# One inverse matmul per frequency instead of two: the filter product crossed over by VectorE and summed on GpSimd

## The chip, the cores and the metric

The kernel runs on one core of a Trainium2 chip. The metric is the device time of one execution in microseconds (us), the lower the better. Most executions of a kernel agree within 0.3%. A ratio in this text is the mean time of one kernel's fast runs over the mean of the other's fast runs of the same rounds, so it is not quite the ratio of the medians quoted beside it.

PE is TensorE's matmul stream, PEld its weight loads, DVE is VectorE, ACT is ScalarE, POOL is GpSimd, SP is the queue that issues most DMAs.

## The reference

Two parts in a row: a frequency-domain filter along the sequence, then a feed-forward block with a scaled sigmoid gate.

```python
# x: (8, 3008, 256), filt_r and filt_i: (1505, 256)
X = np.fft.rfft(x, axis=1)
Y = X * (filt_r + 1j * filt_i)
y = np.fft.irfft(Y, n=3008, axis=1)            # (8, 3008, 256)
h = y.reshape(24064, 256) @ w_in               # 2048 columns
g = h / (1 + np.exp(-beta * h))
out = g @ w_out                                # (24064, 256)
```

## The kernel before

The transform of length 3008 = 47 x 64 is done with matmuls in four stages per batch: s1 (47-point), s2 (64-point, with twiddles), the filter product and s3 (inverse 64-point), s4 (inverse 47-point). A complex number lies as real part in partitions 0 to 63 and imaginary part in 64 to 127.

Batch 0 is transformed alone. From then on the feed-forward matmuls of batch b-1 are the main stream, in 752 steps (two w_in matmuls of 512 columns, four w_out matmuls of 256), and the units of batch b's transform are sprinkled into it by a fixed plan.

```python
hpsum = tile_pool(bufs=2, PSUM); opsum = tile_pool(bufs=3, PSUM)   # w_in result; output accumulators
fpsum = tile_pool(bufs=3, PSUM)                                    # all transform results
...
def s2(i):                                   # two frequencies, 2*i and 2*i+1
    ps = fpsum.tile([P, 2, D], F32)
    # two matmuls of 256 columns into ps, weights t2
    p_t = pqpool.tile([P, 2, D], BF16)
    q_t = pqpool.tile([P, 2, D], BF16)
    nc.vector.tensor_tensor(p_t[:], ps[:], fr_sb[:, k0 : k0 + 2, :], ALU.mult)
    nc.vector.tensor_tensor(q_t[:], ps[:], fi_sb[:, k0 : k0 + 2, :], ALU.mult)
def s3(i):
    ps = fpsum.tile([P, 2, D], F32)
    for e in range(2):                       # two matmuls per frequency, summed in PSUM
        for tab, src, first in ((t3p, p_t, True), (t3q, q_t, False)):
            nc.tensor.matmul(ps[:, e, :], lhsT=tab[...], rhs=src[:, e, :], start=first, stop=not first)
    evac(st["z"][:, kk : kk + 2, :], ps[:], both)   # ScalarE in batch 0, else VectorE
def s23(i):
    if i < NK // 2: s2(i)()
    if i >= 1:      s3(i - 1)()
...
spans = ((0.0, 0.20), (0.32, 0.60), (0.74, 1.0))   # shares of a batch's steps for s1, s2+s3, s4
...
for s in range(len(steps) + LAG):
    # w_in matmuls of step s; gate on ScalarE
    # the transform units planned for step s
    # w_out matmuls of step s-2 into acc; after 16 steps (a block of 512 tokens):
    nc.vector.tensor_copy(ost[...], acc[h][...])   # two copies of 128x512
```

The table t3q holds the same weights as t3p, turned by a quarter and with the sign of the conjugated half. That is how the cross terms of the complex product get to the right half and sign: the second matmul does it.

## Time and profile before

888.59 us (median of the 4 runs beside the changed kernel, 887.69 to 890.02).

| engine | busy us | share of 885.9 us |
|---|---|---|
| PE | 783.4 | 88% |
| ACT | 543.2 | 61% |
| DVE | 414.1 | 47% |
| POOL | 38.2 | 4% |

The page of the profile: the busy line, the busy tenths in 40 equal slices for PE and VectorE, and the chain that ended last with its first line by source.

```profile
span 885.9 us, 14752 instructions
PE 783.4 (88%) x5860; PEld 551.3 (62%) x5953; DVE 414.1 (47%) x691; ACT 543.2 (61%) x789; POOL 38.2 (4%) x79
...
PE   0023599999999999999999999999999999999997
...
DVE  6844556545463438335563437435463438331101
...
PE 77%; DMA 14%; DVE 4%; issue 2%; ACT 1%; SPq 1%; DVEq 0%; ACTq 0%
```

From about 110 us PE is at 90% or more to the end, and the chain is PE for 77%. So the body is bound by the matmul stream. VectorE's 47% is an average over stages, and its slices go up and down between 3 and 8 as long as there are transforms. The stage that the change touches is looked at alone in the next two views, for batch 3. First the timeline of VectorE (start us, us, engine, line, operation, shapes; in brackets the idle time in front of it):

```profile
337.44 0.69 DVE L333 TENSOR_TENSOR p_t<-ps_3530,fr_sb 128x512 bf16<-128x512 f32 x1 [0.50 <-PE ps_3530 L324]
338.05 0.68 DVE L334 TENSOR_TENSOR q_t<-ps_3530,fi_sb 128x512 bf16<-128x512 f32 x1
338.64 0.68 DVE L282 CAST z<-ps_3537 128x512 bf16<-128x512 f32 x1
339.83 0.69 DVE L333 TENSOR_TENSOR p_t<-ps_3562,fr_sb 128x512 bf16<-128x512 f32 x1 [0.50 <-PE ps_3562 L324]
```

An instruction takes 0.68 us, but the next one starts 0.60 us after it: they overlap by 0.08. A unit of this stage is one pair of frequencies: its products on VectorE and one z copy. A unit comes every 2.39 us, VectorE needs 1.8 to 1.9 of it and idles 0.50. It has some room here, not half of its time. Second, the waits of PE between 329 and 371 us, this stage (who waited for whom: us in total, times, longest):

```profile
PE ps_3427 L324 <- DMA a_3320<-d_3048: 0.8, 1, 0.8
PE acc L474 <- DVE ost L486: 0.2, 1, 0.2
```

PE waits for nothing of VectorE's but 0.2 us.

### The profile page before, as it was taken

How to read it: one execution, taken by the hardware profiler on the slowest of the kernel's cores; microseconds unless marked ns; L12 is line 12 of the kernel's file. 1: busy time of each engine (PE TensorE's matmuls, PEld its weight loads, DVE VectorE, ACT ScalarE, POOL GpSimd, SP SyncE). 2: the span in 40 equal slices, each digit the busy share in tenths (PEclk: the TensorE clock that was granted, in tenths of full speed). 3: DMA queues.
4: the chain of work that ended last, by engine and by line, in shares of the span. 5: the costliest groups of instructions: out<-in, count | busy, mean ns of one | idle time of the engine just before them, and what ended most of it. 6: DMA issues, size and time to landing. Idle time of an engine off the chain costs nothing.

```text
span 885.9 us, 14752 instructions
## 1 busy us (share of the span) xinstructions
PE 783.4 (88%) x5860; PEld 551.3 (62%) x5953; DVE 414.1 (47%) x691; ACT 543.2 (61%) x789; POOL 38.2 (4%) x79
## 2 busy tenths in 40 slices
PE   0023599999999999999999999999999999999997
PEld 0001466676676767677676767777676767777665
DVE  6844556545463438335563437435463438331101
ACT  1311365666667665776667665676667665777775
POOL 5010010001000000001000000000000000000000
PEclk9999799999999999999999999999999999999999
DMA  9967465517523382507524371504523152501011
GB/s 212 221 146 182 125 120 159 137 37 155 148 85 112 64 197 62 154 26 156 147 79 119 63 198 61 155 26 112 155 79 106 56 150 62 153 26 48 25 48 48
DMA packets 94869, 97.70 MB, mean 110 GB/s; under 512 B 6544, under 2 KB 84880, under 8 KB 94800
## 3 DMA queue, kind: packets, MB, share of 16 engines
q1 hardware_dynamic: 90432, 83.38, 31.5%
q0 software_dynamic: 4368, 13.37, 10.4%
q8 instruction: 46, 0.75, 0.3%
q14 instruction: 23, 0.19, 0.1%
HBM read 60.30 MB, written 49.81 MB: 124 GB/s over the span
## 4 chain that ended last, share of the span: by engine, by line
PE 77%; DMA 14%; DVE 4%; issue 2%; ACT 1%; SPq 1%; DVEq 0%; ACTq 0%
PE acc L474 34%; PE hps L440 31%; DMA fr_sb<-in_filt_r_dram 5%; DVE ost L486 2%; DMA ws<-in_moe_w_out_dram 1%; DMA d_676<-a_738 1%; DMA d_1769<-a_1985 1%; DMA d_3048<-a_3264 1%; DMA d_5606<-a_5822 1%; DVE q_t L334 1%; DMA d_319<-a_347 1%; DMA zz<-d_677 1%; DMA d_676<-a_838 1%; DMA d_319<-a_375 1%; SPq L259 1%
## 5 line engine op out<-in xcount | busy, mean ns | idle before, releaser
L449 ACT ACTIVATE gT<-hps,beta_sb 128x512 bf16<-128x512 f32 x752 | 515.8, 687 | 252.6 <-PE hps L440 217.4
L474 PE MATMUL acc<-wout_sb,gT 128*128 128x256 bf16 x3008 | 456.7, 273 | 5.1 <-DVE ost L486 0.9
L440 PE MATMUL hps<-y,win_sb 128*128 128x512 bf16 (+7 forms) x1635 | 429.6, 351 | 0.5 <-DVE y L284 0.3
L474 PEld LDWEIGHTS <-gT 128*128 128x128 bf16 x3008 | 287.2, 98 | 143.3 <-issue 6.8
L440 PEld LDWEIGHTS <-win_sb 128*128 128x128 bf16 x1728 | 165.0, 98 | 25.6 <-issue 1.7
L486 DVE COPY ost<-acc 128x512 f32<-128x512 f32 x94 | 60.2, 681 | 123.1 <-PE acc L474 123.0
L386 PEld LDWEIGHTS <-zz 96*128 96x128 bf16 x512 | 36.5, 102 | 35.5 <-DMA zz<-d_320 7.7
L303 PEld LDWEIGHTS <-t_129 94*96 94x96 bf16 x128 | 16.7, 132 | 58.3 <-issue 53.1
L324 PEld LDWEIGHTS <-t_131 128*128 128x128 bf16 x192 | 19.2, 100 | 40.6 <-issue 20.9
L80 POOL DMA_DIRECT2D xg<-in_x_dram x32 | 17.2, 536 | 570.2 <-PE ps_6948 L303 85.1
L303 PE MATMUL ps_343<-xg,t_129 94*96 94x512 bf16 x1 | 0.6, 586 | 31.2 <-ACT a_333 L280 31.2
L349 PEld LDWEIGHTS <-t3q 128*128 128x128 bf16 x192 | 19.1, 99 | 8.7 <-issue 5.6
L349 PEld LDWEIGHTS <-t3p 128*128 128x128 bf16 x192 | 19.1, 99 | 5.7 <-DVE p_t L333 0.8
L81 POOL DMA_DIRECT2D xg<-in_x_dram x32 | 16.4, 513 | 1.6 <-DMA xg<-in_x_dram 1.6
L303 PE MATMUL ps_351<-xg,t_129 94*96 94x512 bf16 x1 | 0.6, 586 | 14.8 <-DVE a_333 L282 14.8
L137 DVE TENSOR_TENSOR r<-u,r 128x1536 f32<-128x1536 f32 x6 | 10.5, 1758 | 0.2
L280 ACT ACTIVATE a_347<-ps_351 96x512 bf16<-96x512 f32 x1 | 0.6, 592 | 16.1 <-PE ps_351 L303 16.1
L165 PE MATMUL tp<-ident,t_129 94*96 94x94 bf16 x1 | 0.3, 312 | 11.3 <-DVE t_129 L161 11.3
L138 ACT ACTIVATE t_131<-r 128x1536 bf16<-128x1536 f32 x2 | 3.0, 1483 | 10.7 <-DVE r L137 10.7
L324 PE MATMUL ps_397<-a_389,t_131 128*128 128x256 bf16 x2 | 0.6, 397 | 9.0 <-DMA a_389<-d_319 9.0
L264 DVE TENSOR_SCALAR wout_sb<-ws,rbeta_sb 128x256 bf16<-128x256 f32 x16 | 4.6, 348 | 7.7 <-DMA ws<-in_moe_w_out_dram 7.7
L138 ACT ACTIVATE t3p<-r 128x1536 bf16<-128x1536 f32 x2 | 3.0, 1483 | 7.5 <-DVE r L137 7.5
(1158 smaller groups left out, 622.3 us busy)
## 6 DMA issues: line engine op xcount, KB each, us to landing
out_dram<-ost SPq DMA_DIRECT2D x47, 512.0 KB, 2.9
xg<-in_x_dram POOLq DMA_DIRECT2D x32, 320.0 KB, 5.3
fr_sb<-in_filt_r_dram SPq DMA_DIRECT2D x16, 192.0 KB, 6.9
fi_sb<-in_filt_i_dram SPq DMA_DIRECT2D x16, 192.0 KB, 8.6
ws<-in_moe_w_out_dram SPq DMA_DIRECT2D x4, 512.0 KB, 5.9
xg<-in_x_dram POOLq DMA_DIRECT2D x32, 56.0 KB, 5.6
d_320<-z SPq DMA_DIRECT2D x4, 384.0 KB, 2.7
zz<-d_320 SPq DMA_DIRECT2D x4, 384.0 KB, 5.5
```

The lines of the kernel that those rows point to most:

```text
L80: nc.gpsimd.dma_start(t[:80], xv[:80, js, :])
L81: nc.gpsimd.dma_start(t[80:NP], xv[80:NP, js, :])
L137: nc.vector.tensor_tensor(r, u, r, ALU.subtract)
L259: nc.sync.dma_start(ws[:], moe_w_out[f0 * P : (f0 + WG) * P, :].rearrange("(fb fp) j -> fp fb j", fp=P),)
L303: nc.tensor.matmul(ps[:KP], lhsT=t1[:], rhs=xg[g][:, jj : jj + 2, :], start=True, stop=True)
L324: nc.tensor.matmul(ps[:, e, :], lhsT=t2[:, k0 + e, :, :].rearrange("p c k -> p (c k)"), rhs=st["a2"][g][:, kk + e, :], start=True, stop=True,)
L349: nc.tensor.matmul(ps[:, e, :], lhsT=tab[:, k0 + e, :, :].rearrange("p c k -> p (c k)"), rhs=src[:, e, :], start=first, stop=not first,)
L386: nc.tensor.matmul(ps[:, e, :NP], lhsT=zz[:, j0 % JG + e, dc * P : (dc + 1) * P], rhs=t4[:], start=True, stop=True,)
L440: nc.tensor.matmul(hps[:, pos - t0 : pos - t0 + ln], lhsT=win_sb[:, dc, fb * P : (fb + 1) * P], rhs=ys[b][:, dc, n0 : n0 + ln], start=(dc ...
L449: nc.scalar.activation(gT[:, :tn], hps[:, :tn], ACT.Silu, scale=beta_sb[:, fb : fb + 1])
L474: nc.tensor.matmul(acc[tb // 2][:, tb % 2, :], lhsT=gT[:, tb * P : (tb + 1) * P], rhs=wout_sb[:, fb, :], start=(fb == 0 and tb % 2 == 0), ...
L486: nc.vector.tensor_copy(ost[:, 2 * h : 2 * h + n, :], acc[h][:, :n, :])
```

## The change

The intent is to take one of the two inverse matmuls per frequency off the bound engine. The two products are summed before the matmul, on GpSimd, which is idle. For that the cross terms must already lie in the right half, so VectorE writes them there: two products of 64 partitions, each reading one half and writing the other, with the sign as a per-partition scalar. The table t3q and its set-up go. Since GpSimd adds latency, s3 runs three units behind s2 in place of one.

```diff
-                p_t = pqpool.tile([P, 2, D], BF16, name="p_t", tag="p_t")
-                q_t = pqpool.tile([P, 2, D], BF16, name="q_t", tag="q_t")
+                p_t = pqpool.tile([P, 2, D], F32, name="p_t", tag="p_t")
+                q_t = pqpool.tile([P, 2, D], F32, name="q_t", tag="q_t")
+                v_t = vpool.tile([P, 2, D], BF16, name="v_t", tag="v_t")
                 nc.vector.tensor_tensor(p_t[:], ps[:], fr_sb[:, k0 : k0 + 2, :], ALU.mult)
-                nc.vector.tensor_tensor(q_t[:], ps[:], fi_sb[:, k0 : k0 + 2, :], ALU.mult)
+                for lo, to in ((0, M), (M, 0)):
+                    nc.vector.scalar_tensor_tensor(
+                        q_t[to : to + M], ps[lo : lo + M], sgn[lo : lo + M],
+                        fi_sb[lo : lo + M, k0 : k0 + 2, :], ALU.mult, ALU.mult,
+                    )
+                nc.gpsimd.tensor_tensor(v_t[:], p_t[:], q_t[:], ALU.add)
...
                 for e in range(2):
-                    for tab, src, first in ((t3p, p_t, True), (t3q, q_t, False)):
-                        nc.tensor.matmul(ps[:, e, :], lhsT=tab[...], rhs=src[:, e, :], start=first, stop=not first)
+                    nc.tensor.matmul(ps[:, e, :], lhsT=t3p[...], rhs=v_t[:, e, :], start=True, stop=True)
...
-                if i >= 1:
-                    s3(i - 1)()
+                if i >= VLAG:                 # VLAG = 3
+                    s3(i - VLAG)()
...
-            n = (J // 2, NK // 2 + 1, J // 4 * NDC)[k]
+            n = (J // 2, NK // 2 + VLAG, J // 4 * NDC)[k]
```

Cut: the pool of v_t (four buffers), the set-up of sgn in place of t3q, and a scaling of fi_sb's first row that t3q carried before. Some calls are joined onto one line.

More of the change, by code (lines that the diff above doesn't have):

```diff
@@ L28 @@
 NK = 24
+VLAG = 3
 J = 32
@@ L109 @@
     t3p = consts.tile([P, NK, 2, M], BF16, name="t3p", tag="t3p")
-    t3q = consts.tile([P, NK, 2, M], BF16, name="t3q", tag="t3q")
+    sgn = consts.tile([P, 1], F32, name="sgn", tag="sgn")
     beta_sb = consts.tile([P, NFB], F32, name="beta_sb", tag="beta_sb")
@@ L230 @@
         )
-        for t3, base, extra in ((t3p, 1, False), (t3q, 2, True)):
-            for c2 in range(2):
-                off = small(f"o3{base}{c2}")
-                nc.vector.tensor_scalar(
-                    off[:], cq[:], 0.25 * (base - c2), None, ALU.add
-                )
-                if extra:
-                    nc.vector.tensor_tensor(off[:], off[:], hs[:], ALU.add)
-                nc.vector.tensor_scalar(u[:], w[:], off[:], None, ALU.add)
-                reduce_sin(t3[:, :, c2, :], u[:], r[:])
-        nc.vector.tensor_scalar_mul(t3q[:, 0, :, :], t3q[:, 0, :, :], keep[:])
+        for c2 in range(2):
+            off = small(f"o3{c2}")
+            nc.vector.tensor_scalar(off[:], cq[:], 0.25 * (1 - c2), None, ALU.add)
+            nc.vector.tensor_scalar(u[:], w[:], off[:], None, ALU.add)
+            reduce_sin(t3p[:, :, c2, :], u[:], r[:])
+        s2_ = small("s2_")
+        nc.vector.tensor_scalar(s2_[:], c_p[:], -2.0, 1.0, ALU.mult, ALU.add)
+        nc.vector.tensor_scalar(sgn[:], hs[:], -4.0, 1.0, ALU.mult, ALU.add)
+        nc.vector.tensor_tensor(sgn[:], sgn[:], s2_[:], ALU.mult)
+        nc.vector.tensor_scalar_mul(fi_sb[:, 0, :], fi_sb[:, 0, :], keep[:])
         beta_src = moe_beta.rearrange("(fb fp) -> fp fb", fp=P)
@@ L269 @@
     pqpool = ctx.enter_context(tc.tile_pool(name="pqpool", bufs=2))
+    vpool = ctx.enter_context(tc.tile_pool(name="vpool", bufs=4))
     zpool = ctx.enter_context(tc.tile_pool(name="zpool", bufs=2))
@@ L330, in go @@
                     )
-                p_t = pqpool.tile([P, 2, D], BF16, name="p_t", tag="p_t")
-                q_t = pqpool.tile([P, 2, D], BF16, name="q_t", tag="q_t")
+                p_t = pqpool.tile([P, 2, D], F32, name="p_t", tag="p_t")
+                q_t = pqpool.tile([P, 2, D], F32, name="q_t", tag="q_t")
+                v_t = vpool.tile([P, 2, D], BF16, name="v_t", tag="v_t")
                 nc.vector.tensor_tensor(p_t[:], ps[:], fr_sb[:, k0 : k0 + 2, :], ALU.mult)
-                nc.vector.tensor_tensor(q_t[:], ps[:], fi_sb[:, k0 : k0 + 2, :], ALU.mult)
-                st["pq", i] = (p_t, q_t)
+                for lo, to in ((0, M), (M, 0)):
+                    nc.vector.scalar_tensor_tensor(
+                        q_t[to : to + M],
+                        ps[lo : lo + M],
+                        sgn[lo : lo + M],
+                        fi_sb[lo : lo + M, k0 : k0 + 2, :],
+                        ALU.mult,
+                        ALU.mult,
+                    )
+                nc.gpsimd.tensor_tensor(v_t[:], p_t[:], q_t[:], ALU.add)
+                st["v", i] = v_t
             return go
@@ L344, in go @@
                     st["z"] = zpool.tile([P, KG, D], BF16, name="z", tag="z")
-                p_t, q_t = st.pop(("pq", i))
+                v_t = st.pop(("v", i))
                 ps = fpsum.tile([P, 2, D], F32, name="ps3", tag="f")
                 for e in range(2):
-                    for tab, src, first in ((t3p, p_t, True), (t3q, q_t, False)):
-                        nc.tensor.matmul(
-                            ps[:, e, :],
-                            lhsT=tab[:, k0 + e, :, :].rearrange("p c k -> p (c k)"),
-                            rhs=src[:, e, :],
-                            start=first,
-                            stop=not first,
-                        )
+                    nc.tensor.matmul(
+                        ps[:, e, :],
+                        lhsT=t3p[:, k0 + e, :, :].rearrange("p c k -> p (c k)"),
+                        rhs=v_t[:, e, :],
+                        start=True,
+                        stop=True,
+                    )
                 evac(st["z"][:, kk : kk + 2, :], ps[:], both)
@@ L399, in fft_units @@
             [s1(i) for i in range(J // 2)],
-            [s23(i) for i in range(NK // 2 + 1)],
+            [s23(i) for i in range(NK // 2 + VLAG)],
             [s4(i) for i in range(J // 4 * NDC)],
```

## The prediction

> **What bounds it now.** The busy table gives PE 783 of 886 us, DVE 414, ACT 543, POOL 38. After a start-up of about 110 us the slices show PE at 90% or more to the end, at full clock, and the list of PE's waits holds almost nothing after start-up (about 10 us in all). So the body is bound by the PE stream and the start-up by waits: filter and w_out loads until 60 us, then the transform of batch 0 with nothing to hide it.
>
> **Removed.** One of two inverse-stage matmuls per frequency: 24 per batch. In the timeline these start 0.108 us apart: 2.6 us a batch, 18 us over batches 1 to 7, which run inside the PE stream. Two t3q tables also go (about 9 us of DVE and ACT in set-up), but the chain of waits shows start-up held by loads until 60 us, and VectorE only then turns to its stage-1 copies behind the w_out scaling. Gain there: 0.
>
> **Added.** Per pair of frequencies VectorE has three PSUM reads in place of two: the half-height products have 512 elements a partition each, so each costs like a full one. The group list has the 128x512 product at 0.68 to 0.69 us, 0.60 start to start, the z copy the same. scalar_tensor_tensor with a pointer scalar was 0.06 us longer than tensor_tensor at 96 columns (0.32 against 0.26), so I estimate 0.74 each. The Trainium skill (VectorE: DVE Perf Modes, "Two Vector instructions with no wait between them") says that an instruction whose start quadrant differs from the one before starts only when all earlier ones have finished; the two halves switch quadrants, so the 0.08 us of overlap should be lost in all of them. No trace here shows it yet. VectorE then needs about 2.95 us per pair with the z copy (2.5 if the overlap stays), against 1.8 to 2.0 before.
>
> GpSimd's 128x512 fp32 add: the skill (GPSIMD Engine Reference, section 3.1) has 4497 ns at 2048 columns, so an estimate of 1.2 us. It is under VectorE's pace and three units of lag cover it. Not a bound.
>
> **On the critical path.** Units of this stage lie 1.9 matmul steps apart now (15 units in 0.28 of about 93 steps), 0.86 us a step: PE needs about 2.04 us per unit, VectorE 2.95. Before it was 2.4 against 2.0. The three transform PSUM buffers let PE run only about one unit ahead, so PE stalls. Per batch, VectorE: 3 x 2.3 + 9 x 2.95 + 1.8 of output copies = 35 us; PE: 24 us. About one unit of lead and tail leaves a stall of 8 to 10 us (5 without lost overlap), against 2.6 saved. Batches 1 to 7: +21 to +50 us. Batch 1 has a shorter window: +3.
>
> Batch 0: VectorE sets the pace there (12 pairs in 15.9 us). At 2.0 to 2.27 us a pair and GpSimd's latency at the end: +9 to +12 us.
>
> Sum: 889 + 30 to 65. I expect 940 us, range 910 to 962. Faster by over 2%: 0.03; within 2%: 0.09; slower: 0.88.
>
> **What would show it.** PE busy down about 20 us, but PE waiting 40 us or more in the filter stage for transform PSUM buffers released by the VectorE products or z copies; VectorE at 90% or more there; its products 0.7 us or more start to start; GpSimd adds near 1.2 us and hardly waited for; batch 0's filter stage near 26 us in place of 16.
>
> **What would make it wrong.** Half-height products that cost half, or overlap as before; PE with more room ahead of VectorE than three buffers suggest; or a GpSimd add above 3 us or contending with VectorE, which would be slower still.

## The result, and the profile after

965.37 us (963.36 to 967.11, 4 runs) against 888.59: ratio 1.086 (95% interval 1.083 to 1.089). The change makes the kernel slower by 8.6%. The direction was predicted, the size was not: 940 was expected, with 962 as the upper end.

The same lines of the page after, with those groups that are new or that wait:

```profile
span 962.1 us, 14714 instructions
PE 783.5 (81%) x5674; PEld 531.8 (55%) x5761; DVE 502.4 (52%) x780; ACT 540.5 (56%) x787; POOL 160.4 (17%) x175
...
PE   0024497799879997899869997899969997899997
...
DVE  6437457735592439534593448734593439531011
...
PE 59%; DVE 23%; DMA 11%; issue 5%; SPq 1%; ACT 0%; POOL 0%; DVEq 0%; POOLq 0%; ACTq 0%
...
L486 PE MATMUL acc<-wout_sb,gT 128*128 128x256 bf16 x3008 | 461.8, 274 | 28.1 <-DVE ost L498 24.3
...
L347 POOL TENSOR_TENSOR v_t<-p_t,q_t 128x512 bf16<-128x512 f32 x96 | 121.7, 1268 | 313.3 <-DVE q_t L339 313.3
```

PE now dips once per batch, where VectorE peaks, and VectorE has gone from 4% to 23% of the chain. GpSimd's add takes 1.27 us and waits for VectorE all the time; it holds nobody up in the body. Note the line of the w_out matmuls: they wait 24.3 us for the copies of the output accumulators, which the change does not touch.

VectorE's timeline in the same stage of batch 3:

```profile
379.77 0.69 DVE L285 CAST z<-ps_3646 128x512 bf16<-128x512 f32 x1
380.49 0.69 DVE L337 TENSOR_TENSOR p_t<-ps_3668,fr_sb 128x512 f32<-128x512 f32 x1
381.20 1.51 DVE L339 SCALAR_TENSOR_TENSOR q_t<-ps_3668,sgn,fi_sb 64x512 f32<-64x512 f32 x2
382.75 0.69 DVE L285 CAST z<-ps_3678 128x512 bf16<-128x512 f32 x1
```

A unit repeats after 2.98 us (379.77 to 382.75) and there is no idle time in it. A product of 64 partitions takes 0.75 us, no less than one of 128, and each of these four starts only when the one before has finished: 0.71 to 0.79 us apart in place of 0.60. PE's waits between 360 and 412 us:

```profile
PE acc L486 <- DVE ost L498: 3.9, 2, 2.7
PE ps_3646 L361 <- DVE q_t L339: 1.5, 1, 1.5
PE ps_3589 L361 <- DVE q_t L339: 1.1, 1, 1.1
...
PE ps_3621 L361 <- DVE q_t L339: 0.6, 1, 0.6
```

So there are two kinds of wait: for a transform PSUM tile that VectorE's products still hold, and for an output accumulator whose copy stands behind those products in VectorE's queue. The place of the longest one, in the timeline of PE and VectorE:

```profile
389.89 0.38 PE L486 MATMUL acc<-wout_sb,gT 128*128 128x256 bf16 x2
390.11 1.51 DVE L339 SCALAR_TENSOR_TENSOR q_t<-ps_3766,sgn,fi_sb 64x512 f32<-64x512 f32 x2
391.65 0.69 DVE L285 CAST z<-ps_3776 128x512 bf16<-128x512 f32 x1
...
392.26 1.28 DVE L498 COPY ost<-acc 128x512 f32<-128x512 f32 x2
393.00 0.38 PE L486 MATMUL acc<-wout_sb,gT 128*128 128x256 bf16 x2 [2.72 <-DVE ost L498]
```

After it the granted clock drops: the trace has it at 0.50 from 393.9 to 397.3 us. The stretch from 393 to 397 us (busy us of each engine, then the mean granted clock, DMA share, GB/s):

```profile
393.00:397.00 4.00, 4.00 (x19) 2.52 (x19) 3.34 (x5) 1.37 (x2) 0.53 (x2) 0.61 0.41 133
```

Batch 0 is its own case, as it has no matmul stream. Its first and last product, before and then after:

```profile
79.97 0.69 DVE L333 TENSOR_TENSOR p_t<-ps_397,fr_sb 128x512 bf16<-128x512 f32 x1 [9.59 <-PE ps_397 L324]
...
95.18 0.68 DVE L334 TENSOR_TENSOR q_t<-ps_541,fi_sb 128x512 bf16<-128x512 f32 x1
```

```profile
76.73 0.69 DVE L337 TENSOR_TENSOR p_t<-ps_390,fr_sb 128x512 f32<-128x512 f32 x1 [9.82 <-PE ps_390 L327]
...
102.32 1.51 DVE L339 SCALAR_TENSOR_TENSOR q_t<-ps_537,sgn,fi_sb 64x512 f32<-64x512 f32 x2
```

That is 15.9 us before and 27.1 after for twelve pairs.

Where the 76.2 us between the two spans lie, measured in the two traces from the first filter product of a batch to its first s4 copy (the stage) and between:

| part | before | after | difference |
|---|---|---|---|
| start to the first product of batch 0 | 80.0 | 76.7 | -3.2 |
| stage of batch 0 | 24.4 | 36.8 | +12.4 |
| stages of batches 1 to 7 | 290.5 | 355.5 | +65.0 |
| the rest | 491.0 | 493.0 | +2.0 |

The first row is scatter of the loads: the changed kernel's unaltered start-up also gave 79 to 81 us in the profiles below. The third row adds up as follows. Saved matmuls: 168 x 0.108 = -18 us. Waits of PE as they are drawn: 44.3 us in 50 waits for transform tiles (summed before rounding) and 24.3 in 13 waits for output copies, +68 against before. Clock: the lost share (time multiplied by one minus the granted clock, from 120 us on) is 8.5 us against 1.7, so +7. That makes 57. The other 8 us lie in how waits are drawn: a pair of 256-column matmuls is drawn 0.38 us long though the next one can start after 0.22, so each of the 63 waits looks 0.16 us shorter than it is. Counted from start to start of PE's matmuls, less 0.11 us for 256 columns and 0.22 for 512, the same waits are 52.5 us and 26.4 us (1.7 for output copies before), and the clock outside of them costs 6 us more than before. -18 + 52.5 + 24.7 + 6 is 65, the whole row.

### The profile page after: what moved, and what is told of

It reads as the page before. It is cut to its first block, busy times and chain, and to the rows that moved or that the text cites. A ratio compares the mean times of both kernels' runs of the same rounds, so it can differ in the third digit from the quotient of the medians.

```text
span 962.1 us, 14714 instructions
## 1 busy us (share of the span) xinstructions
PE 783.5 (81%) x5674; PEld 531.8 (55%) x5761; DVE 502.4 (52%) x780; ACT 540.5 (56%) x787; POOL 160.4 (17%) x175
## 4 chain that ended last, share of the span: by engine, by line
PE 59%; DVE 23%; DMA 11%; issue 5%; SPq 1%; ACT 0%; POOL 0%; DVEq 0%; POOLq 0%; ACTq 0%
PE acc L486 27%; PE hps L452 25%; DVE q_t L339 10%; DVE p_t L337 6%; DVE z L285 4%; DMA fr_sb<-in_filt_r_dram 3%; DVE ost L498 3%; DMA ws<-in_moe_w_out_dram 1%; DMA d_5659<-a_5875 1%; SPq L261 1%; DMA d_312<-a_340 1%; DMA zz<-d_682 1%; DMA d_681<-a_843 1%; DMA a_3353<-d_3077 1%; DMA d_312<-a_368 1%
## 5 line engine op out<-in xcount | busy, mean ns | idle before, releaser
L486 PE MATMUL acc<-wout_sb,gT 128*128 128x256 bf16 x3008 | 461.8, 274 | 28.1 <-DVE ost L498 24.3
L347 POOL TENSOR_TENSOR v_t<-p_t,q_t 128x512 bf16<-128x512 f32 x96 | 121.7, 1268 | 313.3 <-DVE q_t L339 313.3
L361 PEld LDWEIGHTS <-t3p 128*128 128x128 bf16 x192 | 15.3, 100 | 75.9 <-issue 32.0
L283 ACT ACTIVATE z<-ps_431 128x512 bf16<-128x512 f32 x1 | 0.6, 598 | 14.6 <-PE ps_431 L361 14.6
```

What stands on the lines that cost most here:

```text
L347: nc.gpsimd.tensor_tensor(v_t[:], p_t[:], q_t[:], ALU.add)
L486: nc.tensor.matmul(acc[tb // 2][:, tb % 2, :], lhsT=gT[:, tb * P : (tb + 1) * P], rhs=wout_sb[:, fb, :], start=(fb == 0 and tb % 2 == 0), ...
```

## The experiments

### e1: three products, no change of quadrant

```diff
-                for lo, to in ((0, M), (M, 0)):
-                    nc.vector.scalar_tensor_tensor(q_t[to : to + M], ps[lo : lo + M], sgn[lo : lo + M], fi_sb[lo : lo + M, ...], ...)
+                q2_t = pqpool.tile([P, 2, D], F32, name="q2_t", tag="q2_t")
+                for dst in (q2_t, q_t):
+                    nc.vector.scalar_tensor_tensor(dst[:], ps[:], sgn[:], fi_sb[:, ...], ...)
```

> Wrong result on purpose: the two half-height products become two full-height ones, each from all 128 partitions to the same 128 partitions (one into an unread tile). Still three VectorE products of 512 columns per pair, but no start quadrant changes. Theory (VectorE sets the pace of the filter stage, and half of the extra is the lost overlap of held instructions): products start 0.61 to 0.67 us apart in place of 0.71 to 0.77, unit about 2.55 us in place of 2.97; 0.42 us x 12 units x 7 batches = 35 us, plus 4 us in batch 0: 915 to 932 us. Rival (the quadrants play no part; three products or the pointer scalar cost this by themselves): spacing unchanged, 958 to 970 us.

Measured: 925.55 us, 40 less than the change; the result is wrong. VectorE's timeline of this kernel:

```profile
357.33 0.68 DVE L337 TENSOR_TENSOR p_t<-ps,fr_sb 128x512 f32<-128x512 f32 x1
357.93 1.40 DVE L340 SCALAR_TENSOR_TENSOR q_t<-ps,sgn,fi_sb 128x512 f32<-128x512 f32 x2
359.25 0.68 DVE L285 CAST z<-ps 128x512 bf16<-128x512 f32 x1
359.84 0.68 DVE L337 TENSOR_TENSOR p_t<-ps,fr_sb 128x512 f32<-128x512 f32 x1
```

The unit is 2.51 us in place of 2.98 with three products all the same. The spacing is 0.60 and 0.66 again. So crossing the halves costs 0.47 us per unit by itself, because none of the four instructions overlaps its neighbour; it is half of the 76 us. The edit takes away the half height and the crossing together with the change of quadrant; what tells them apart is said in the account of the prediction below.

### e2: one cross product, the rest of the change kept

```diff
-                for lo, to in ((0, M), (M, 0)):
-                    nc.vector.scalar_tensor_tensor(q_t[to : to + M], ps[lo : lo + M], ...)
+                nc.vector.scalar_tensor_tensor(q_t[:], ps[:], sgn[:], fi_sb[:, ...], ...)
```

> Wrong result on purpose: one full-height product without crossing in place of the two half-height ones; the rest of the change (GpSimd add, lag of three units, one inverse matmul per frequency) stays. Theory (only the third VectorE product and the quadrant switch cost time): unit about 1.9 us, below PE's 2.04, so no stall: 889 less 18 for the matmuls, plus 1 for GpSimd's latency in batch 0: 866 to 880 us, PE waits in the filter stages under 1 us a batch. Rival (the GpSimd add, the lag, or the three transform PSUM tiles cause the stall): at least 900 us.

Measured: 885.04 us, wrong result; ratio to before 0.996. The rival falls: GpSimd's add, the lag and the tiles cost no 80 us. But the range of the theory is missed by 5 us, and that taught something. The stages of batches 2 to 7 are 41.2 to 41.6 us against 42.1 before, so a batch gains under 1 us of the 2.6 that the matmuls are worth. With two products VectorE has 1.9 us of work in a unit of 2.1 to 2.2, and an output copy now comes late: in the body PE waits 9.1 us in 8 waits for output copies (0.9 before). Batch 0's stage is 27.7 us against 24.4, from the longer product (0.66 us apart) and GpSimd's latency at the end. The stages of batches 1 to 7 together are 6.8 us shorter than before: 18 for the matmuls, less 8 more of waits for output copies and 3 for transform tiles. So even without the third product the copy's place in VectorE's queue took nearly half of the saving.

### e3: z copies on ScalarE

```diff
-                evac(st["z"][:, kk : kk + 2, :], ps[:], both)
+                evac(st["z"][:, kk : kk + 2, :], ps[:], True)
```

> Correct result: the z copy of all batches goes to ScalarE, which is 56% busy. Theory: VectorE's unit falls from 2.97 to 2.27 us, its stage from 36.6 to about 30 us against PE's 24; the stall falls from about 11 us a batch to 4 or 5, and fewer drops of the clock: 905 to 925 us. Rival (PE waits for the number of transform PSUM tiles or for GpSimd, not for VectorE's total): under 10 us gained, 955 or more.

Measured: 928.52 us, correct; 37 gained, 4 us over the range. The waits for transform tiles are nearly gone (1.6 us in place of 44), but the waits for output copies have grown from 24.3 to 31.0 us and the lost clock share from 8.5 to 13.7 us. As I read it, PE runs further ahead of VectorE with its tiles free sooner, and then stands longer at the end of the block (3.5 us at most, in place of 2.7). The wait has moved rather than shrunk by the amount of work taken away.

### e4: output copies on ScalarE

```diff
-                    nc.vector.tensor_copy(ost[...], acc[h][:, :n, :])
+                    nc.scalar.activation(ost[...], acc[h][:, :n, :], ACT.Copy)
```

> Correct result: the copies of the output accumulators go to ScalarE. Theory (the output copy queues behind VectorE's backlog, PE waits 2.7 us for it once a batch and loses the lead that three transform tiles give it, and the clock then drops for 3 us): the wait of the w_out matmuls for the copy falls from 24 us to under 3, no drop of the clock in the filter stages, 925 to 940 us. Rival (only VectorE's total time counts, the place of the wait is nothing of its own): 1.3 to 2.6 us a batch gained, 945 to 957 us.

Measured: 936.08 us, correct; 29 gained, within the range of the theory and outside the rival's. PE's waits for VectorE and for the copies from 115 us on:

```profile
PE ps L361 <- DVE q_t L339: 45.7, 55, 1.9
PE acc L486 <- ACT ost L498: 3.6, 14, 0.5
```

The first kind of wait stays, and only the second goes (3.6 us in place of 24.3). The lost clock share is 1.7 us, as before the change. The stages are 47.1 us in place of 52.0. VectorE's output copies at the two block ends where PE waits are 2.6 us of work. If these count in full, about 2.3 us per batch come from the place of the copy in the queue and the clock, not from VectorE's total.

### e5: a wider stage in the plan

```diff
-        spans = ((0.0, 0.20), (0.32, 0.60), (0.74, 1.0))
+        spans = ((0.0, 0.13), (0.25, 0.73), (0.86, 1.0))
```

> Correct result: only the plan changes. The filter stage takes 0.48 of the matmul steps of a batch in place of 0.28, stages 1 and 4 take 0.13 and 0.14, so PE has about 3.2 us a unit for VectorE's 2.97. Theory (VectorE is short of time only locally; it is about half busy over the whole run): nearly all of the stall of batches 1 to 7 goes, though VectorE's work is the same: 883 to 900 us, about 12 us of it batch 0, some waits for output copies left. Rival (VectorE's work as such, or its latency, costs the time): 940 us or more.

Measured: 940.9 us, correct. The theory is missed by 40 us, and the rival's number came out. But the rival's reason did not: the waits of PE between 330 and 440 us in this kernel are

```profile
PE acc L486 <- DVE ost L498: 5.5, 4, 2.4
PE ps L306 <- DVE a L285: 2.9, 2, 1.6
PE ps L327 <- DMA a<-d: 0.8, 1, 0.8
```

No wait for the products is among them (0.8 us in the whole body), and VectorE idles about 2 us after each block end. What is left is the wait for output copies, 38.5 us in 26 waits, more than in the change itself. A unit is 2.2 to 3.0 us of VectorE's work in one piece; a copy that comes behind it waits for all of it, however idle VectorE is on average, and a wider stage meets more block ends. The clock follows: lost share 18.8 us. The stretch behind one such wait of 2.4 us:

```profile
380.50:383.60 3.10, 3.04 (x16) 1.86 (x16) 1.01 (x3) 1.38 (x2) 0.12 (x1) 0.69 0.90 279
```

### e6: z and output copies on ScalarE, plan unchanged

The edits of e3 and e4 together.

> Correct result: z copies and output copies both go to ScalarE, plan unchanged. Theory (the z copy alone gained 37 us and left 31 us of waits for output copies behind VectorE's products): VectorE then has 12 x 2.25 = 27 us per stage against PE's 28 at the last unit; waits for output copies under 4 us in all, stages of 40 to 42 us in place of 46 to 52: 880 to 895 us. Rival (the gains of e3 and e4 overlap, or ScalarE becomes the next bound): 905 us or more.

Measured: 893.03 us, correct; ratio to before 1.004. The stages of batches 2 to 7 are 40.7 to 40.8 us. The waits for output copies are 4.6 us in 20 waits, a little over the 4 that was expected. ScalarE is 69% busy and no new bound.

### e7: wider stage and output copies on ScalarE

The edits of e4 and e5 together.

> Correct result: the wider filter stage of e5 and the output copies on ScalarE. Theory: no stall by VectorE left in batches 2 to 7, so 889 less 18 (matmuls) plus about 12 (batch 0) plus 2 to 4 (short window of batch 1): 882 to 890 us, VectorE waits of PE under 1 us a batch from batch 2 on. If the saved matmuls are worth less than 0.108 us each: above 895.

Measured: 884.9 us, correct; ratio 0.997. Against e5 only the engine of the output copies differs, and that is 56 us. From e5 to e7 the waits for output copies fall by 34.9 us in the profiles, the lost clock share by 18.8. VectorE still does the three products and the z copy of every unit here, one unit in 3.04 us. The waits between 330 and 440 us:

```profile
PE ps L306 <- DVE a L285: 1.0, 1, 1.0
PE ps L327 <- DMA a<-d: 0.5, 1, 0.5
PE acc L486 <- ACT ost L498: 0.5, 2, 0.2
```

From one batch's first s4 copy to the next (batches 1 to 7) it takes 93.7 to 97.1 us, against 96.6 to 102.1 before. Five of the six intervals are 2.1 to 3.0 us shorter than before; the sixth is 5.7 shorter, since the kernel before waits 2.0 us for a DMA in it. The 2.6 us per batch that the removed matmuls promised are there once nothing else waits. What keeps e7 from being faster than before is batch 0, whose stage is 37.2 us.

### e8: as e7, batch 0 in the old form

```diff
+                if b == 0:
+                    nc.vector.tensor_tensor(pb[:], ps[:], fr_sb[:, k0 : k0 + 2, :], ALU.mult)
+                    nc.vector.tensor_tensor(qb[:], ps[:], fi_sb[:, k0 : k0 + 2, :], ALU.mult)
+                    st["v", i] = (pb, qb)
+                    return
...
+                    pairs = ((t3p, v_t[0]), (t3q, v_t[1])) if b == 0 else ((t3p, v_t),)
```

with t3q built as before, and a lag of one unit in batch 0.

> Correct result: as e7, but batch 0, which has no matmul stream to hide behind, uses the old form (two products, two matmuls, lag of one unit). Theory: batch 0's filter stage returns from about 27 to 16 us, end to end 10 to 13 us less than e7: 870 to 878 us, faster than both kernels. Rival (batch 0's loss is hidden by other start-up waits): within 4 us of e7.

Measured: 873.87 us (868.81 to 877.92), correct; ratio to before 0.984 (0.978 to 0.989). Batch 0's stage is 23.5 us in place of 37.2. It is the fastest kernel, 11 us below e7, and about 1.6% faster than before with an interval that excludes 1.

### e9: the kernel before with the remedies of e7

The edits of e4 and e5 applied to the kernel before.

> Correct result: the kernel before with the two remedies of e7 (wider filter stage, output copies on ScalarE), two products and two matmuls as before. Theory (the kernel before waits for VectorE almost nowhere after start-up, so the remedies have nothing to remedy there): 884 to 892 us, the same as before. Rival (the gain of e8 comes from the plan and the copies, not from the saved matmuls): 878 us or less.

Measured: 887.7 us (881.08 to 893.58), correct; ratio 0.997 (0.993 to 1.001). The remedies by themselves gain nothing where VectorE holds nobody up.

### e10: the matmul given back

```diff
+                    if b > 0:
+                        pairs = pairs * 2          # the second matmul overwrites with the same values
```

> Correct result: e8 with each inverse matmul of batches 1 to 7 issued twice (the second overwrites the first with the same values), so only the saved PE work is given back. Theory (0.108 us each, all on the critical path once VectorE has room): 168 x 0.108 = 18 us over e8, 889 to 896 us. Rival (the saving is hidden or was never real): within 6 us of e8.

Measured: 883.54 us, correct, 10.5 us over e8's second run on the same chip. Both ranges are missed: the saving is real, but less came back than 18 us. In the profiles the middle batches take 98.8 to 99.1 us from one first s4 copy to the next, against 96.4 to 96.9 in e8 except for one interval of 98.4. That is 2.2 to 2.7 us a batch where nothing else disturbs, as expected. From batch 0's first s4 copy to batch 7's it takes 674.1 us in e10, 659.8 in e8 and 661.5 in e11, the second run of e8's kernel. So 12.6 to 14.3 of the 18 us come back in this stretch. In the body PE waits 10.3 us in e10 against 14.0 in e8 and 13.7 in e11, so 3 to 4 us of the added work seem to fill waits that were there anyway. Besides, the profiled run of e10 began its first s4 copy 2.8 us earlier than e8's and 1.1 us earlier than e11's, which is scatter of the start-up. These two cover most of the missing 7 us.

### e11: e8 once more

> The kernel of e8 again with five rounds, on the same chip as e9 and e10: 868 to 878 us, ratio to before 0.98 to 0.99. A ratio above 0.995 would mean that e8 was a lucky draw.

Measured: 873.06 us, correct; ratio to before 0.984 (0.981 to 0.987). e8 was no lucky draw. On this chip it is 14.6 us below e9, which has the same plan and the same output copies but the old filter stage in all batches.

## Why the prediction was right and wrong

**Right: what the change does to VectorE.** The prediction had 0.74 us for a half-height product and 2.95 us per unit; the trace has 0.75 and 2.98. That the overlap of neighbours is lost rested on the Trainium skill (VectorE: DVE Perf Modes, "Two Vector instructions with no wait between them"). This case's trace agrees: e1 has 2.51 us per unit without the switch of quadrants. e1 changed the height of the products and the crossing too, so on its own it doesn't tell which of the three counts. Other pairs do. A change of height alone costs no overlap: 96-partition copies of stage 1 and 128-partition output copies, all from partition 0, follow each other after 0.60 to 0.61 us. Nor does holding need half-height neighbours: the z copy at 379.77 and the p_t product behind it both start at partition 0, and still lie 0.72 us apart (0.60 in e1), while the output copy at 392.26 follows the z copy at 391.65 after 0.61 us. The page's rule compares start quadrants separately for SBUF and PSUM, with the last instruction that used that memory. The z copy reads nothing from SBUF, so p_t is compared with the q_t product before it, which read fi_sb from partition 64. The output copy reads nothing from SBUF, and is not held.

**Right: GpSimd is no bound.** The estimate of 1.2 us from the skill (GPSIMD Engine Reference, section 3.1) measured 1.27, in all 96 adds between 1.261 and 1.274 us. e2, e6 and e7 keep the add and have hardly a wait for it in the body (at most 0.5 us).

**Right: batch 0.** The products take 11 us more there (15.9 to 27.1), the stage 12.4; 9 to 12 was predicted. e7 against e8 gives 11 us end to end.

**Signs.** Of the signs that the prediction named, the waits for transform tiles came (44 us), and VectorE was 94% busy from 360 to 397 us. PE's busy time did not fall by 20 us: it is 783.5 us against 783.4. It counts matmuls at the length at which they are drawn, also at half clock, so it is no measure of what was saved; the sum was not worked out.

**Right in kind: matmuls saved.** About 2.6 us per batch show up in e7, and 2.2 to 2.7 came back in e10's undisturbed batches.

**Wrong: the stall.** The step that failed reads: "About one unit of lead and tail leaves a stall of 8 to 10 us (5 without lost overlap), against 2.6 saved. Batches 1 to 7: +21 to +50 us." The stages of batches 1 to 7 measured +65 us, which is a stall of 11.9 us a batch before the 2.6 saved. The kind of wait was right, its size was not, and a second wait was missing. Three things stand in its place.

- The case that keeps the overlap did not come. The lower half of the range, and with it the 940 in the middle, was a hedge between two cases, of which e1 shows the first to be real, worth 40 us over the whole run.
- The lead of one unit was counted as kept to the end of the stage. It is not: the stage contains a block end, where PE needs an output accumulator whose copy stands behind the products in VectorE's in-order queue. The prediction counted the copies as 1.8 us of work and overlooked that they are a second way for VectorE to hold PE. PE waited 24.3 us for them in the run. e4 takes the copies away and has stages of 47.1 us, that is 7.6 above 42.1 - 2.6 = 39.5: about the stall that the prediction had computed (with the copies' 1.8 us in it). With the copies in VectorE's queue it is 12.5 (52.0).
- After four of the six longest waits (2.7 us) the granted clock falls to 0.50 for 3.4 us. The lost share is 7 us more than before; e4, e6 and e7, which have no such waits, have 1.7 us or none of it. The prediction had taken the clock of the body as full.

**My theory between the runs fell once.** After e4, I still thought that VectorE was merely short of time in the stage, and that a wider stage would be enough. e5 gave it the time and stayed at 941. Only with the output copies out of VectorE's queue (e7, 885) was the time worth anything. So here the queue position of a short, urgent copy behind a long burst was a cost of its own, beside the total of the work.

Left open: the last 2 us or so by which e10 fell short of 18, and whether another PSUM tile for the transform results or the output accumulators would have shortened PE's waits, which no run tried. A version that crosses the halves and still overlaps was not found.

## What to carry to other kernels

Before moving work off the bound engine, compute what the helper engine needs per unit in the very stage where it lands, with start-to-start times, and compare it with the pace that the bound engine will have after the change, which is faster than today's. Then list everything else that goes through the helper's in-order queue and that the bound engine needs, since a copy of 0.6 us behind a burst of 3 us made PE wait up to 2.7 us here, even with VectorE half idle (e5). Where the hidden batches gain from a form that the exposed first batch loses with, use both forms.

## What the Trainium skill lacked or had wrong

- VectorE: DVE Perf Modes, "Two Vector instructions with no wait between them", calls its rule a model and gives no cost. Here it held for products that read one 64-partition half and write the other, and for the full-height p_t product behind the z copy. It cost 0.47 us in a unit of four instructions (2.98 against 2.51): start to start 0.71 to 0.79 us in place of 0.60 to 0.66.
- The same page has no figure for scalar_tensor_tensor with a per-partition scalar and a PSUM source: 0.74 to 0.75 us at 512 columns of fp32, against 0.68 to 0.69 for tensor_tensor, and the same for 64 as for 128 partitions.
- TensorE: Matmul & The Clock Gate, Part 1, lets the clock drop to half after an idle window of about 3.4 us and calls the window free-running. The free-running window agrees: all 92 clock changes in the 13 traces lie on one grid of 3.413 us in each trace. But a window need not be idle throughout. Of 2949 windows at full clock, counted from start to start as above, none with under 2.1 us of idle was followed by a drop, and all 30 with 2.2 us or more were. So a wait of 2.7 us drops the clock or not by how it lies on the grid: the two such waits in the changed kernel that dropped nothing left at most 2.12 us of idle in one window.
- GPSIMD Engine Reference, section 3.1, has the add measured at 2048 columns only (4497 ns). At 512 columns of fp32 with a bf16 result it took 1.27 us, 13% over a quarter of that (1.12 us). The 96 adds differ by 13 ns, so there is no sign of contention with the products running beside them on VectorE.
- No page that I read warns that a short copy behind a burst of other work in the queue of a half-idle engine can hold PE: 38.5 us of waits in e5, and 56 us end to end between e5 and e7.
